# Attention and two dense layers on one core: GpSimd is taken out of layer 1's second product, tiles are lent to whoever comes first

## The chip, the cores and the metric

The kernel runs on one core of a Trainium2 chip. The metric is the device time of one execution in microseconds (us), as the median of a few runs. TensorE (PE, with its weight loads as PEld), VectorE (DVE), ScalarE (ACT), GpSimd (POOL) and the DMA queue that SyncE (SP) feeds work side by side, each through its own list of instructions in a fixed order, with semaphores between them.

## The reference

```
scores = q @ k.T / 8, plus a decay from the running sum of log f, causal mask
x  = softmax(scores) @ v            # 4 batches, 8 heads, 576 rows, 64 columns -> x is 2304 x 512
h  = x @ w_in;   g  = max(0.01 h, h)       # layer 1: w_in 512 x 2048
x1 = g @ w_out                             # layer 1's second product: w_out 2048 x 512
h2 = x1 @ wi2;   g2 = h2 * sigmoid(h2)     # layer 2, same shapes
out = g2 @ wo2
```

The four weights come as 64-bit floats and are turned into 32-bit ones on the chip.

## The kernel before, in words

Each product is made in a split form: an fp32 operand becomes a rounded high part (a copy on ACT) and a low part, operand minus high part (a subtraction), and three matmuls sum high*high, high*low and low*high. The three products behind layer 1's first one also use Strassen's scheme with seven products, numbered q = 1 to 7, so that sums and differences of quarters ("mixes") are made ahead of the split.

No order is written out by hand. A planner (class Plan) runs the kernel's generators in an estimated time: each step asks for an engine with an estimated cost and a rank, each engine takes the waiting step of the lowest rank, and each issue adds one instruction to that engine's list. What two engines can do goes to the one that the planner expects to be done first (either, L137); engines "pd" means POOL or DVE, "d" DVE alone. A subtraction of over 256 columns on POOL is issued as two pieces (less, L337). The chip then works through the lists; only the data decide the waits.

The stretch that the change touches, layer 1's second product, is made of these parts:

- quarters (L1048) loads quarters of g from DRAM (`gq<-g_d`). made (L1088) forms the sums for q 5 and 6 on them (`gq<-gq`, L1328 or, on POOL, L1327), with X_ON the engines of the first. prep (L1099) copies the high part on ACT (L1126) into a tile `gs` and subtracts the low part on DVE (L348), through four `gs` tiles in turn; PE's product reads them (`acc<-gs,w`, L1193, 12 matmuls for each of the 84 `gs`). The three groups of 768 rows are n = 0, 1, 2.
- fills (L1865) loads mixed weights from DRAM (`w<-w_d`, L1882), copies the high part (L1883) and subtracts the low part, `w<-w`, L348 on DVE or L344 on POOL. fills(0) is layer 1's w_out, fills(1) layer 2's wi2, fills(2) its wo2.
- fetch2 (L1841), second_weights (L1896) and combos (L1854) load the raw layer-2 weights (`wst`), turn them into fp32 on ACT and DVE (L1679 to L1683), mix them on DVE (`f<-f`, L1328) in one of two tiles `f`, and store them (`w_d<-f`, L1907). The raw tiles are three `stg` tiles.
- second_input (L1331) loads x1 for layer 2's first product (`x1s`, in an `f` tile, and `x1t`, in two `stg` tiles), mixes it and splits it into `xc`, which `m<-xc,w` (L1491) reads. second_values (L1547) does the same for the last product (`m<-w,gc`, L1634).

An `f` or `stg` tile is taken by a running number (take, L208): number i waits until number i - 2, or i - 3, has been given back, so tiles go round in turn.

Of the kernel before, what the change touches and what calls it, by code (L numbers as in the profile page):

```python
# [19 lines left out]
STG_BUFS = 3  # L20
# [7 lines left out]
U_BUFS = 2  # L28
F_BUFS = 2
MM = 0.119  # L30
# [29 lines left out]
SPLITS = 4  # L60
X_ON = "pd"
SET_B = ("h", "h", ("acc", 0), ("acc", 1))
# [25 lines left out]
class Plan:  # L88
# [8 lines left out]
    def __init__(self):  # L97
        self.now, self.count = 0.0, 0
        self.events, self.ready, self.free = [], {}, {}
        self.seen, self.waiting = {}, {}  # L100
        self.taken, self.given, self.queue = {}, {}, {}
        self.dma_free = 0.0
        self.rate = 360e3
        self.filler = {}

    def at(self, t, fn):
# [113 lines left out]
    def give(self, pool, i):  # L220
        self.given[pool, i] = True
        fn = self.queue.pop((pool, i), None)
        if fn:
            fn()

    def par(self, *gens):
        def step(resume):
            left = [len(gens)]

            def one():  # L230
                left[0] -= 1
                if not left[0]:
                    resume()

            for g in gens:
                self.start(g, one)

        return step
# [28 lines left out]
def fused_kernel(ctx, tc, qt, kt, va, vb, ft, w1, wi2, wo2, out):  # L267
# [49 lines left out]

    def stg(shape, dtype, name):
        return main.tile(shape, dtype, tag="stg", name=name, bufs=STG_BUFS)

# [278 lines left out]
    def load_head(n):  # L599
# [32 lines left out]
        i_st = yield take("stg", STG_BUFS)  # L632
        st = stg([128, S + HALF[1][1]], F32, "qk")
        q2, k2 = st[:, S:S + tn], st[:, 0:ke]
# [573 lines left out]

    last = {}
    split_last = NG * 7 * SF - SPLITS  # L1210

    def sums(n, j, held):
# [35 lines left out]
        if n < NG - 1:  # L1248
            i_u = yield take("u", U_BUFS)
            u = w2t["a"].tile([128, TB], F32, tag="u", name="u", bufs=U_BUFS)  # L1250
        else:
            if j == 0:
                i_u = yield take("f", F_BUFS)
                last["u"] = w2t["b"].tile([128, 2, TB], F32, tag="f", name="us", bufs=F_BUFS)
                signal("last_u")
            yield wait("last_u")
            u = last["u"][:, j]
# [26 lines left out]
        if n < NG - 1:  # L1284
            give("u", i_u)
        elif j == 0:
            yield wait(("x1", n, 0, 3))
            give("f", i_u)

# [41 lines left out]
    def second_input():  # L1331
        yield wait("decoded")
        for g in range(NG):
            yield wait("decoded", *[("x1", g, i, c) for i in range(2) for c in range(KC)])
            if g:
                yield wait(("m", NP * g - STAGE_LEAD[g - 1], 7))
            i_f = yield take("f", F_BUFS)
            signal(("col", g))
            col = w2t["b"].tile([128, 2, 2, TB], F32, tag="f", name="x1s", bufs=F_BUFS)
            a11, a21 = col[:, 0], col[:, 1]  # L1340
            st, st_i = {}, {}

            def load(dst, c, k):
# [4 lines left out]
            def right(k):  # L1348
                st_i[k] = yield take("stg", STG_BUFS)
                st[k] = stg([128, 2, TB], F32, "x1t")  # L1350
                yield from load(st[k], 1, k)

            def split(q, src, done=None):
                t, back = yield from x_room(q)
                xc[g, q] = t, back
                rank = 0 if g or q != 7 else -2
                yield act(2 * TB, lambda: nc.scalar.copy(t[:, 0], src), rank, 0.09)
                yield less(2 * TB, t[:, 1], src, f32(t[:, 0]), "d", rank, PE_LAT)
                if done is not None:
                    give("stg", done)  # L1360
                signal(("xc", g, q))
# [24 lines left out]
            yield wait(*[("xc", g, q) for q in QO])  # L1386
            give("f", i_f)

# [158 lines left out]
    def second_values():  # L1547
        order = [(*tiles2[n], jp) for jp in range(NP // 2) for n in range(2)]
        order += [(*tiles2[n], jp) for n in range(2, len(tiles2)) for jp in range(NP // 2)]
        loaded = {}  # L1550

        def loads2():
            for k in order:
                g, th, jp = k
                yield wait(("g2", g, 2 * jp), ("g2", g, 2 * jp + 1), "wo2_made", ("col", NG - 1))
                i = yield take("f", F_BUFS)
                f = w2t["b"].tile([128, 7, HW], F32, tag="f", name="g2", bufs=F_BUFS)
                yield dma(524e3, lambda: nc.sync.dma_start(
                    out=f[:, 0:4].rearrange("p s (a t) -> p s a t", a=2),
                    in_=g2_d[g, jp, :, :, :, th * 128:(th + 1) * 128]))  # L1560
                loaded[k] = f, i
                signal(("f2", *k))

        p.start(loads2())
        yield wait(("xc", NG - 1, QO[-1]))
        for k in order:
            yield wait(("f2", *k))
            yield from value_combos(*k, *loaded.pop(k))
# [3 lines left out]
    def value_combos(g, th, jp, f, i):  # L1572
# [29 lines left out]
        def back():  # L1602
            yield wait(*[("gc_split", g, th, jp, m) for m in (0, 2, 4, 6)])
            give("f", i)

# [86 lines left out]
    def room(f):  # L1692
# [7 lines left out]
        if where in ("ring0", "ring1"):  # L1700
            t = main.tile(shape, I32, tag=where, name="wsr", bufs=RING_BUFS)
        elif where == "g":
            t = main.tile(shape, I32, tag="g", name="wsg", bufs=G_BUFS)
        elif where == "stg":
            t = stg(shape, I32, "wst")
        else:
            t = slot(where, shape, I32, "wss")
# [133 lines left out]
    def fetch2():  # L1841
        for which in range(2):
            if which:
                yield wait(("m1", NG - 1, 1, 2))
            for j in range(NP):
                for e in range(2):
                    i_st = yield take("stg", STG_BUFS)
                    st = stg([128, DM, 2], I32, "wst")
                    yield dma(524e3, lambda: nc.sync.dma_start(
# [4 lines left out]
    def combos(which, j, f):  # L1854

        y = f[:, 4:6].rearrange("p s n -> p (s n)")
        for e in range(2):
# [3 lines left out]
            yield from to_f32(t, st, y, t, 2, True)  # L1861
            give("stg", i_st)
        yield from mix(f, 2 - which, 2)

    def fills(which):  # L1865
        for u in range(NU):
# [12 lines left out]
            def fill(u, at_, t):  # L1879
# [3 lines left out]
                yield act(2 * HW, lambda: nc.scalar.copy(t[:, :, 0], src), rank)  # L1883
                yield less(2 * HW, t[:, :, 1], src, f32(t[:, :, 0]), "pd", rank, PE_LAT)
                if which == 0:
# [10 lines left out]
    def second_weights():  # L1896
# [3 lines left out]
        def line(which, todo):  # L1900
            while todo:
                j = todo.pop(0)
                yield wait(("words2", which, j, 0))
                i = yield take("f", F_BUFS)
                f = w2t["b"].tile([128, 7, HW], F32, tag="f", name="f", bufs=F_BUFS)
                yield from combos(which, j, f)
# [3 lines left out]
                signal(("spilt", which + 1, j))  # L1910
                give("f", i)

        for which in range(2):
            todo = list(range(NP))
            yield par(*[line(which, todo) for _ in range(F_BUFS)])
        signal("wo2_made")
# [10 lines left out]
    def opening():  # L1927
        first_row["i"] = yield take("stg", STG_BUFS)
        first_row["tile"] = stg([H, 2, HALF[0][1]], F32, "cfr")
        for i in range(5):  # L1930
# [67 lines left out]
```

## Time and profile before

| | before |
|---|---|
| median of three runs | 974.35 us (973.66 to 976.08) |
| profiled execution, its own time | 974.26 us |
| its span, first to last instruction | 972.6 us |
| granted TensorE clock, mean of the span | 0.995 |

In the profile an engine's idle time before an instruction is put down to what released it. Stretches of the span: attention and layer 1's first product to about 392 us (its last matmuls run on to 423 between the others), layer 1's second product from 392 to 619, layer 2's first product from 582 to 794, its second from 794 to 965.

### The profile page before, as it was taken

How to read it: one execution, taken by the hardware profiler on the slowest of the kernel's cores; microseconds unless marked ns; L12 is line 12 of the kernel's file. 1: busy time of each engine (PE TensorE's matmuls, PEld its weight loads, DVE VectorE, ACT ScalarE, POOL GpSimd, SP SyncE). 2: the span in 40 equal slices, each digit the busy share in tenths (PEclk: the TensorE clock that was granted, in tenths of full speed). 3: DMA queues.
4: the chain of work that ended last, by engine and by line, in shares of the span. 5: the costliest groups of instructions: out<-in, count | busy, mean ns of one | idle time of the engine just before them, and what ended most of it. 6: DMA issues, size and time to landing. Idle time of an engine off the chain costs nothing.

```text
span 972.6 us, 18370 instructions
## 1 busy us (share of the span) xinstructions
PE 943.0 (97%) x6483; PEld 891.2 (92%) x6483; DVE 765.3 (79%) x1752; ACT 609.6 (63%) x1382; POOL 127.1 (13%) x126
## 2 busy tenths in 40 slices
PE   9999999999999999899999988999999999999998
PEld 7777998989888989898989978999999999999998
DVE  5998786699689952889899889666656588888885
ACT  6978787788588843665445456456566675444442
POOL 2001220121023100324020157000000020000000
PEclk9999999999999999999999999999999999999999
DMA  7852553466777557894967563695877883544442
GB/s 178 268 174 87 161 172 91 134 229 214 238 235 248 183 184 261 289 375 130 325 216 242 172 219 109 208 335 171 309 273 243 282 266 114 152 131 136 144 122 77
DMA packets 160024, 196.81 MB, mean 202 GB/s; under 512 B 9638, under 2 KB 145982, under 8 KB 159900
## 3 DMA queue, kind: packets, MB, share of 16 engines
q1 hardware_dynamic: 159500, 195.24, 62.8%
q8 instruction: 51, 0.84, 0.4%
q10 hardware_dynamic: 432, 0.39, 0.1%
q14 instruction: 41, 0.34, 0.1%
HBM read 125.94 MB, written 69.65 MB: 201 GB/s over the span
## 4 chain that ended last, share of the span: by engine, by line
PE 71%; DVE 13%; DMA 7%; ACT 4%; issue 3%; SPq 1%; POOL 0%; DVEq 0%; ACTq 0%; POOLq 0%
PE m L1491 18%; PE m L1634 18%; PE hpw L935 12%; PE acc L1193 11%; PE sps L718 4%; PE av L867 4%; PE tps L799 3%; DVE gs L348 2%; DMA gq<-g_d 2%; DVE gq L1328 2%; DVE sc L698 1%; ACT sc L741 1%; PE hps L935 1%; DMA wsr<-in_w_dram 1%; ACT sc L751 1%
## 5 line engine op out<-in xcount | busy, mean ns | idle before, releaser
L935 PE MATMUL hpw<-ring,w 128*128 128x320 f32 (+1 forms) x1344 | 217.4, 303 | 0.1
L1193 PE MATMUL acc<-gs,w 128*128 128x384 f32 x1008 | 187.0, 344 | 13.2 <-DVE gs L348 6.4
L1193 PEld LDWEIGHTS acc<-gs,w 128*128 128x128 f32 x1008 | 180.7, 191 | 16.9 <-DVE gs L348 8.1
L935 PEld LDWEIGHTS hpw<-ring,w 128*128 128x128 f32 x1344 | 190.4, 190 | 2.4 <-issue 1.4
L1491 PE MATMUL m<-xc,w 128*128 128x384 f32 x1008 | 181.4, 340 | 3.8 <-ACT ev L1234 2.0
L1491 PEld LDWEIGHTS m<-xc,w 128*128 128x128 f32 x1008 | 178.1, 188 | 5.4 <-ACT ev L1234 2.3
L1634 PE MATMUL m<-w,gc 128*128 128x256 f32 x1512 | 178.6, 280 | 0.0
L1634 PEld LDWEIGHTS m<-w,gc 128*128 128x128 f32 x1512 | 178.4, 188 | 0.0
L333 ACT CAST gc<-g 128x512 fp32r<-128x512 f32 (+1 forms) x180 | 80.6, 490 | 86.1 <-DVE g L1328 54.9
L1126 ACT CAST gs<-gq 128x768 fp32r<-128x768 f32 x84 | 69.4, 836 | 72.1 <-DVE gq L1328 35.8
L741 ACT ACTIVATE sc<-sc,st 128x576 f32<-128x576 f32 (+4 forms) x160 | 92.9, 581 | 24.8 <-DVE st L698 23.9
L348 DVE TENSOR_TENSOR gs<-gq,gs 128x768 fp32r<-128x768 f32 x84 | 89.8, 1079 | 21.2 <-ACT gs L1126 20.6
L344 POOL TENSOR_TENSOR w<-w 128x256 fp32r<-128x256 f32 x50 | 60.0, 1227 | 296.1 <-ACT w L1883 296.1
L348 DVE TENSOR_TENSOR gc<-g,gc 128x512 fp32r<-128x512 f32 (+1 forms) x180 | 91.3, 532 | 3.2 <-ACT gc L333 2.1
L698 DVE CUSTOM_DVE_ANT_0 sc<-sps,zmask 128x288 f32<-128x288 f32 (+4 forms) x160 | 71.0, 448 | 28.5 <-PE sps L718 21.2
L344 POOL TENSOR_TENSOR m<-qk,m 64x288 fp32r<-64x288 f32 (+1 forms) x56 | 50.3, 909 | 276.1 <-ACT m L333 129.1
L1328 DVE TENSOR_TENSOR g<-g 128x256 f32<-128x256 f32 x144 | 59.3, 421 | 17.9 <-DMA g<-g_d 17.3
L799 PE MATMUL tps<-ident,sc 66*107 66x66 f32 (+3 forms) x480 | 68.5, 269 | 3.5 <-ACT sc L751 1.9
L718 PE MATMUL sps<-m,s 66*128 66x288 f32 (+9 forms) x288 | 66.8, 313 | 2.1 <-DVE st L698 1.4
L799 PEld LDWEIGHTS tps<-ident,sc 66*107 66x107 f32 (+3 forms) x480 | 55.0, 151 | 11.3 <-ACT sc L751 3.9
L1028 ACT ACTIVATE gw<-hpw 128x320 f32<-128x320 f32 (+1 forms) x112 | 44.6, 408 | 27.9 <-PE hpw L935 24.0
L1883 ACT CAST w<-w 128x512 fp32r<-128x512 f32 x84 | 50.6, 618 | 10.2 <-DMA w<-w_d 9.7
(126 smaller groups left out, 1179.8 us busy)
## 6 DMA issues: line engine op xcount, KB each, us to landing
w<-w_d SPq DMA_DIRECT2D x84, 256.0 KB
gq<-g_d SPq DMA_DIRECT2D x48, 384.0 KB
g_d<-z SPq DMA_DIRECT2D x24, 768.0 KB
g<-g_d SPq DMA_DIRECT2D x36, 512.0 KB
w_d<-f SPq DMA_DIRECT2D x16, 896.0 KB
g_d<-gw SPq DMA_DIRECT2D x32, 320.0 KB
wst<-in_w_dram SPq DMA_DIRECT2D x17, 512.0 KB
g_d<-gw SPq DMA_DIRECT2D x32, 256.0 KB
```

What stands on the lines that cost most here:

```text
L333: ("act", act_cost(n, base), lambda: nc.scalar.copy(dst, src), 0.0),
L344: nc.gpsimd.tensor_tensor(dst[:, s_], a[:, s_], b[:, s_], op=ALU.subtract)
L348: ("dve", dve_cost(n), lambda: nc.vector.tensor_tensor(dst, a, b, op=ALU.subtract), 0.0),
L698: yield dve(w, lambda: nc.vector.tensor_tensor_reduce(out=sc[0:qn, k0:k0 + w], in0=ps[0:qn], in1=zmask[0:qn, z0:z0 + w], scale=-0.125, sca ...
L718: nc.tensor.matmul(ps[0:qn], ht[x][:, qs], ht[y][:, k0:k0 + w], start=r == 0, stop=r == len(ops) - 1)
L741: yield act(kn, lambda: nc.scalar.activation(sc[0:qn, 0:kn], sc[0:qn, 0:kn], ACTF.Exp, scale=-1.0, bias=st[0:qn, 2 * i + a:2 * i + a + 1], ...
L799: nc.tensor.transpose(ps[0:k1 - k0, o:o + qn], ht["p"][i][0:qn, k0:k1], ident[0:qn, 0:qn])
L935: nc.tensor.matmul(dst, w[:, wi, c * 128:(c + 1) * 128], x(xi, c), start=(first_ and c == 0 and r == 0), stop=(c == KC - 1 and r == 2), sk ...
L1193: nc.tensor.matmul(dst, w[:, e, wi, j * 128:(j + 1) * 128], x[:, xi, e], start=start and s == 0 and e == 0 and r == 0, stop=stop and s == ...
L1328: ("dve", dve_cost(n), lambda: nc.vector.tensor_tensor(dst, a, b, op=op_), 0.0),
L1491: nc.tensor.matmul(dst, w[:, wi, c * 128:(c + 1) * 128], x[:, xi, c], start=start and c == 0 and r == 0, stop=stop and c == 1 and r == 2, ...
L1634: nc.tensor.matmul(banks[b][:, e], t[:, gi, a * 128:(a + 1) * 128], w[:, wi], start=begin and a == 0 and r == 0, stop=jp == NP // 2 - 1 an ...
```

## The change

- POOL gets no work behind attention: X_ON and the subtraction in fills become "d".
- The two `f` tiles and, behind attention, the three `stg` tiles get a name of their own each, and a new pair lend / back gives any free one to the first who asks.
- Raw wo2 (fetch2, which = 1) is loaded from the point where q 3 of group 0's `xc` is split, instead of from q 2 of group 2's product.
- second_input for group 0 starts only when q 5 of group 2's product is done (INPUT_AT); groups 1 and 2 keep `x1t` in the tile of the fourth `gs` slot.
- second_values waits for all seven `xc` of the last group instead of the last one.

```
-F_BUFS = 2
-X_ON = "pd"
+INPUT_AT = 5
+X_ON = "d"
...
+    def lend(self, pool, keys):
+        def step(resume):
+            free, queue = self.lent.setdefault(pool, (list(keys), []))
+            if free:
+                resume(free.pop(0))
+            else:
+                queue.append(resume)
+        return step
+
+    def back(self, pool, key):
+        free, queue = self.lent[pool]
+        if queue:
+            queue.pop(0)(key)
+        else:
+            free.append(key)
...
-    def stg(shape, dtype, name):
-        return main.tile(shape, dtype, tag="stg", name=name, bufs=STG_BUFS)
+    def stg(i, shape, dtype, name):
+        return main.tile(shape, dtype, tag=f"stg{i % STG_BUFS}", name=name)
+
+    def own(shape, dtype, name):
+        k = yield p.lend("stg2", range(STG_BUFS))
+        return stg(k, shape, dtype, name), lambda: p.back("stg2", k)
...
+    def mixed(shape, name):
+        k = yield p.lend("f", range(2))
+        return w2t["b"].tile(shape, F32, tag=f"f{k}", name=name), lambda: p.back("f", k)
...
     def second_input():
         yield wait("decoded")
         for g in range(NG):
+            if g == 0:
+                yield wait(("m1", NG - 1, 0, INPUT_AT))
...
-            i_f = yield take("f", F_BUFS)
+            col, i_f = yield from mixed([128, 2, 2, TB], "x1s")
...
+            if g:
+                st["x1t"] = tagged(9, [128, 2, 2, TB], F32, "x1t")
...
-                st_i[k] = yield take("stg", STG_BUFS)
-                st[k] = stg([128, 2, TB], F32, "x1t")
+                if g:
+                    st[k], st_i[k] = st["x1t"][:, k], None
+                else:
+                    st[k], st_i[k] = yield from own([128, 2, TB], F32, "x1t")
...
-        yield wait(("xc", NG - 1, QO[-1]))
+        yield wait(*[("xc", NG - 1, q) for q in QO])
...
     def fetch2():
         for which in range(2):
             if which:
-                yield wait(("m1", NG - 1, 1, 2))
+                yield wait(("xc", 0, 3))
             for j in range(NP):
                 for e in range(2):
-                    i_st = yield take("stg", STG_BUFS)
-                    st = stg([128, DM, 2], I32, "wst")
+                    st, i_st = yield from own([128, DM, 2], I32, "wst")
...
-                yield less(2 * HW, t[:, :, 1], src, f32(t[:, :, 0]), "pd", rank, PE_LAT)
+                yield less(2 * HW, t[:, :, 1], src, f32(t[:, :, 0]), "d", rank, PE_LAT)
```

The other places where an `f` tile is taken (us, g2, f) go through mixed in the same way.

The order of PE stays as it was but for one group of six L1193 matmuls that moves ahead of the first L1491 group. What moves is shown at three places. The changed kernel is some 30 lines longer: its L373 is L348 of before, L1357 is L1328, L1713, L1714 and L1716 are L1680, L1681 and L1683, L1091, L1376, L1914 and L1255 are L1066, L1344, L1882 and L1225, L1567 is L1533.

DVE at the beginning of layer 1's second product (`gq<-gq` are the sums of quarters, `w_5656` is the first filled weight, which PE's first product needs), before and then now:

```order
L348 TENSOR_TENSOR gs<-gq,gs 128x768 x4
L1328 TENSOR_TENSOR gq<-gq 128x768 x6
L1680 TENSOR_SCALAR f<-f 128x512
L1681 SCALAR_TENSOR_TENSOR f<-f 128x512
L348 TENSOR_TENSOR w_5656<-w_5656 128x2x256
L1683 SCALAR_TENSOR_TENSOR f<-wst,f 128x512
```

```order
L373 TENSOR_TENSOR gs<-gq,gs 128x768 x4
L1357 TENSOR_TENSOR gq<-gq 128x768 x8
L373 TENSOR_TENSOR w_5656<-w_5656 128x2x256
L1713 TENSOR_SCALAR f<-f 128x512
L1714 SCALAR_TENSOR_TENSOR f<-f 128x512
L373 TENSOR_TENSOR w_5663<-w_5663 128x2x256
```

DVE has eight sums here instead of six and two on POOL, and the first weight's subtraction stands right behind them.

SP around the loads of x1 for group 0 (`x1s`, `x1t`; `x_d<-u` is group 1's last store of x1, `w_d<-f` a store of mixed wi2), before and then now:

```order
L1849 DMA wst<-in_wi_dram 128x1024
L1344 DMA x1s<-x_d 128x2x384 x2
L1907 DMA w_d<-f 128x1792
L1066 DMA gq<-g_d 128x2x384 x2
L1225 DMA x_d<-ev 128x384
```

```order
L1255 DMA x_d<-u 128x384 x2
L1091 DMA gq<-g_d 128x2x384 x3
L1914 DMA w_7237<-w_d 128x2x256
L1091 DMA gq<-g_d 128x2x384
L1914 DMA w_7255<-w_d 128x2x256
L1914 DMA w_7273<-w_d 128x2x256
L1376 DMA x1s<-x_d 128x2x384 x2
L1376 DMA x1t<-x_d 128x2x384 x2
L1914 DMA w_7291<-w_d 128x2x256
```

The four loads now stand behind the last `gq` load and behind the first wi2 weights, some twenty rows later, in one piece.

DVE around the last `gs` subtractions (`w_7341` and so on are wi2 weights, `z<-m,z` is layer 2's first product), before and then now:

```order
L1328 TENSOR_TENSOR x1t<-x1t,x1s 128x768
L348 TENSOR_TENSOR gs<-gq,gs 128x768
L348 TENSOR_TENSOR xc<-x1s,xc 128x768
L348 TENSOR_TENSOR w_7543<-w_7543 128x2x256
L348 TENSOR_TENSOR gs<-gq,gs 128x768
L348 TENSOR_TENSOR xc<-x1t,xc 128x768 x2
L348 TENSOR_TENSOR w_7582<-w_7582 128x2x256
```

```order
L1357 TENSOR_TENSOR x1t<-x1t,x1s 128x768
L373 TENSOR_TENSOR gs<-gq,gs 128x768
L373 TENSOR_TENSOR xc<-x1s,xc 128x768
L373 TENSOR_TENSOR gs<-gq,gs 128x768
L373 TENSOR_TENSOR w_7320<-w_7320 128x2x256
L373 TENSOR_TENSOR w_7341<-w_7341 128x2x256
L373 TENSOR_TENSOR w_7360<-w_7360 128x2x256
L373 TENSOR_TENSOR xc<-x1t,xc 128x768 x2
L373 TENSOR_TENSOR w_7377<-w_7377 128x2x256
```

Half of the subtractions that POOL did before now stand on DVE ahead of its last `gs`, and half behind it.

## Rows read from the trace of the kernel before

**Rows 1.** The page: busy time by engine, and the chain that ended last.
```profile
PE 943.0 (97%) x6483; PEld 891.2 (92%) x6483; DVE 765.3 (79%) x1752; ACT 609.6 (63%) x1382; POOL 127.1 (13%) x126
...
PE 71%; DVE 13%; DMA 7%; ACT 4%; issue 3%; SPq 1%; POOL 0%; DVEq 0%; ACTq 0%; POOLq 0%
```

**Rows 2.** Windows: stretch and length, engines' busy us (x instructions), clock, DMA share, GB/s.
```profile
392.00:423.00 31.00, 27.11 (x164) 26.77 (x164) 26.21 (x40) 18.50 (x35) 4.63 (x5) 0.94 0.93 306
423.00:451.00 28.00, 26.15 (x146) 25.25 (x144) 25.29 (x25) 18.98 (x31) 15.69 (x12) 1.00 0.66 239
451.00:495.00 44.00, 40.70 (x216) 39.55 (x216) 39.61 (x58) 21.14 (x33) 5.19 (x2) 0.96 0.74 245
495.00:575.00 80.00, 79.94 (x452) 79.84 (x453) 70.90 (x90) 42.06 (x63) 10.51 (x9) 1.00 0.72 232
575.00:619.00 44.00, 36.07 (x190) 34.17 (x189) 39.47 (x40) 26.80 (x44) 26.07 (x21) 0.96 0.36 111
619.00:794.00 175.00, 174.99 (x1000) 174.35 (x999) 111.79 (x201) 108.87 (x208) 3.24 (x4) 1.00 0.81 272
794.00:972.60 178.60, 174.60 (x1485) 174.40 (x1484) 148.26 (x346) 80.00 (x182) 2.08 (x2) 1.00 0.44 131
...
567.00:608.40 41.40, 33.47 (x176) 31.85 (x175) 41.29 (x36) 26.24 (x44) 32.38 (x26) 0.96 0.46 140
```

**Rows 3.** Timeline of PE, 370 to 630: start, length, instructions [idle before <-releaser].
```profile
396.52 1.65 PE L1193 MATMUL acc<-gs,w 128*128 128x384 f32 x4 [3.49 <-DVE w L348]
...
451.33 33.97 PE L1193 MATMUL acc<-gs,w 128*128 128x384 f32 x191 [1.77 <-DVE gs L348]
486.57 0.44 PE L1193 MATMUL acc<-gs,w 128*128 128x384 f32 x1 [1.26 <-ACT gs L1126]
...
577.00 2.38 PE L1193 MATMUL acc<-gs,w 128*128 128x384 f32 x12 [1.11 <-DVE gs L348]
580.95 1.14 PE L1193 MATMUL acc<-gs,w 128*128 128x384 f32 x5 [1.57 <-DVE gs L348]
...
584.10 1.97 PE L1491 MATMUL m<-xc,w 128*128 128x384 f32 x5 [1.83 <-DVE xc L348]
...
594.68 8.74 PE L1193 MATMUL acc<-gs,w 128*128 128x384 f32 x48 [1.44 <-ACT ev L1264]
605.40 1.33 PE L1491 MATMUL m<-xc,w 128*128 128x384 f32 x6 [1.97 <-ACT ev L1234]
```

**Rows 4.** Groups: busy us, mean ns of one; 374.8 to 608.4, then three of 495:535.
```profile
L348 DVE TENSOR_TENSOR gs<-gq,gs 128x768 fp32r<-128x768 f32 x84 | 89.8, 1079 | 21.2 <-ACT gs L1126 20.6
L1328 DVE TENSOR_TENSOR gq<-gq 128x768 f32<-128x768 f32 x43 | 49.4, 1173 | 4.9 <-DMA gq<-g_d 4.6
L348 DVE TENSOR_TENSOR w<-w 128x512 fp32r<-128x512 f32 x29 | 22.8, 804 | 4.4 <-ACT w L1883 4.1
...
L344 POOL TENSOR_TENSOR w<-w 128x256 fp32r<-128x256 f32 x44 | 54.7, 1271 | 110.6 <-ACT w L1883 110.6
...
L348 DVE TENSOR_TENSOR gs<-gq,gs 128x768 fp32r<-128x768 f32 x22 | 20.7, 954 | 2.2 <-ACT gs L1126 1.9
L1328 DVE TENSOR_TENSOR gq<-gq 128x768 f32<-128x768 f32 x8 | 7.4, 951 | 0.0
...
L348 DVE TENSOR_TENSOR w<-w 128x512 fp32r<-128x512 f32 x2 | 1.4, 685 | 0.0
```

**Rows 5.** Timeline 436 to 457, DVE and then POOL.
```profile
445.23 1.49 DVE L348 TENSOR_TENSOR gs<-gq,gs 128x768 fp32r<-128x768 f32 x1
...
450.33 0.95 DVE L348 TENSOR_TENSOR gs<-gq,gs 128x768 fp32r<-128x768 f32 x1
...
438.37 10.35 POOL L344 TENSOR_TENSOR w<-w 128x256 fp32r<-128x256 f32 x8 [4.09 <-ACT w L1883]
```

**Rows 6.** DVE's timeline from 384, and a piece of the chain from 450.
```profile
386.06 8.74 DVE L1328 TENSOR_TENSOR gq<-gq 128x768 f32<-128x768 f32 x6 [4.64 <-DMA gq<-g_d]
...
454.78 4.94 DMA gq<-g_d
```

More of the change, by code (lines that the diff above doesn't have):

```diff
@@ L104, in __init__ @@
         self.filler = {}
+        self.lent = {}
     def at(self, t, fn):
@@ L632, in load_head @@
         i_st = yield take("stg", STG_BUFS)
-        st = stg([128, S + HALF[1][1]], F32, "qk")
+        st = stg(i_st, [128, S + HALF[1][1]], F32, "qk")
         q2, k2 = st[:, S:S + tn], st[:, 0:ke]
@@ L1252, in sums @@
             if j == 0:
-                i_u = yield take("f", F_BUFS)
-                last["u"] = w2t["b"].tile([128, 2, TB], F32, tag="f", name="us", bufs=F_BUFS)
+                last["u"], i_u = yield from mixed([128, 2, TB], "us")
                 signal("last_u")
@@ L1287, in sums @@
             yield wait(("x1", n, 0, 3))
-            give("f", i_u)
+            i_u()
     tiles2 = [(g, th) for g in range(NG) for th in range(TB // 128)]
@@ L1336, in second_input @@
                 yield wait(("m", NP * g - STAGE_LEAD[g - 1], 7))
-            i_f = yield take("f", F_BUFS)
+            col, i_f = yield from mixed([128, 2, 2, TB], "x1s")
             signal(("col", g))
-            col = w2t["b"].tile([128, 2, 2, TB], F32, tag="f", name="x1s", bufs=F_BUFS)
             a11, a21 = col[:, 0], col[:, 1]
             st, st_i = {}, {}
+            if g:
+                st["x1t"] = tagged(9, [128, 2, 2, TB], F32, "x1t")
             def load(dst, c, k):
@@ L1359, in split @@
                 if done is not None:
-                    give("stg", done)
+                    done()
                 signal(("xc", g, q))
@@ L1386, in second_input @@
             yield wait(*[("xc", g, q) for q in QO])
-            give("f", i_f)
+            i_f()
     sets_n = [0]
@@ L1555, in loads2 @@
                 yield wait(("g2", g, 2 * jp), ("g2", g, 2 * jp + 1), "wo2_made", ("col", NG - 1))
-                i = yield take("f", F_BUFS)
-                f = w2t["b"].tile([128, 7, HW], F32, tag="f", name="g2", bufs=F_BUFS)
+                f, i = yield from mixed([128, 7, HW], "g2")
                 yield dma(524e3, lambda: nc.sync.dma_start(
@@ L1603, in back @@
             yield wait(*[("gc_split", g, th, jp, m) for m in (0, 2, 4, 6)])
-            give("f", i)
+            i()
         p.start(back())
@@ L1704, in room @@
         elif where == "stg":
-            t = stg(shape, I32, "wst")
+            t = stg(i, shape, I32, "wst")
         else:
@@ L1861, in combos @@
             yield from to_f32(t, st, y, t, 2, True)
-            give("stg", i_st)
+            i_st()
         yield from mix(f, 2 - which, 2)
@@ L1903, in line @@
                 yield wait(("words2", which, j, 0))
-                i = yield take("f", F_BUFS)
-                f = w2t["b"].tile([128, 7, HW], F32, tag="f", name="f", bufs=F_BUFS)
+                f, i = yield from mixed([128, 7, HW], "f")
                 yield from combos(which, j, f)
@@ L1910, in line @@
                 signal(("spilt", which + 1, j))
-                give("f", i)
+                i()
         for which in range(2):
             todo = list(range(NP))
-            yield par(*[line(which, todo) for _ in range(F_BUFS)])
+            yield par(*[line(which, todo) for _ in range(2)])
         signal("wo2_made")
@@ L1928, in opening @@
         first_row["i"] = yield take("stg", STG_BUFS)
-        first_row["tile"] = stg([H, 2, HALF[0][1]], F32, "cfr")
+        first_row["tile"] = stg(first_row["i"], [H, 2, HALF[0][1]], F32, "cfr")
         for i in range(5):
```

## The prediction

> **What bounds the kernel now.** I read the page first: PE is busy for 97% of the span, and the chain that ended last is 71% PE and 13% DVE [rows 1]. So time can only be won where PE stops, or runs slowly. The windows by stage say where [rows 2]; the reader should compare PE's busy time with the length. From 619 to 794 PE is busy for 174.99 of 175 us, and from 794 on only the end of the kernel is open. From 392 to 619, layer 1's second product, it lacks 3.89, 1.85, 3.30, 0.06 and 7.93 us in the five windows, 17.0 in all. Three of these windows also have a granted clock of 0.94 to 0.96, which is a piece at 1.2 instead of 2.4 GHz: 0.06 of 31, 0.04 of 44 and 0.04 of 44 us, some 5.4 us of lost clock, each time in a window in which PE had stopped. 17.0 + 5.4 = 22.4 us is all that can be won there; an order of PE that hardly changes cannot win elsewhere.
>
> Next PE's timeline, for who ends the stops [rows 3]: nearly all are ended by DVE (first `w`, then `gs`, `xc`), a few by ACT. Behind 567 the reason is plain: DVE is busy for 41.29 of 41.40 us, while PE lacks 7.93 in the window of 44 [rows 2]. DVE is the bound there.
>
> Last, why DVE is so full. In the groups a `gs` subtraction takes 1079 ns on the mean of the stretch and 954 between 495 and 535, where POOL does nothing; a `gq` sum 1173 against 951, a `w` subtraction 804 against 685 [rows 4]. The timeline shows the switch: POOL runs eight pieces back to back from 438.37 to 448.72; a `gs` of DVE takes 1.49 us inside that and 0.95 right behind it [rows 5]. POOL's reads slow DVE. The excess is 84 x 0.125 = 10.5, 43 x 0.222 = 9.5 and 29 x 0.119 = 3.5 us, 23.5 us of DVE's time in the stretch.
>
> **The rule weighed against it.** The rows give a price for a collision: about half a microsecond for one DVE instruction (1.49 - 0.95), and 23.5 us in all [rows 4, 5]. The Trainium skill, "SBUF — State Buffer", section "Who interferes with whom", says that a DVE instruction with two SBUF inputs contends with a GpSimd instruction that reads SBUF, and that the shared port pair is an exclusive lock: the loser fully blocks until the other's instruction ends. That there is contention, the rows confirm; blocked for POOL's mean piece of 1.271 us, 44 times, DVE would lose 56 us, and the relief would be more than PE's stops can return. The rows show less than half of it, and the sum goes by them.
>
> **The change part by part**, against the profiled execution's own 974.26 us (median 974.35, so the two stand for each other).
>
> *Off POOL.* In the stretch POOL does 44 pieces, that is 22 `w` subtractions [rows 4], and 5 `gq` sums (its other 5 instructions of 49). All go to DVE, at 0.685 and 0.951 us [rows 4]: 15.1 + 4.8 = 19.9 us, against 23.5 us of excess that goes. But the order puts only 11 of the 22 ahead of the last `gs`: 7.5 + 4.8 = 12.3 us. It also draws some ten short `f` instructions of wi2 ahead of it, at most 0.685 each, 6.9. So DVE's work ahead of the last `gs` falls by 4 us at least; I take 6 to 8, since `x1s`, `x1t` and `xc` instructions had an excess too. Three more `w` subtractions between 785 and 800 go to DVE: 2.1 us, hidden behind PE's own 174.6 us, DVE being busy for 148.26 of 178.60 [rows 2]; without that cover 2.1 us.
>
> *First stop* (3.49 before 396.52, ended by `w` [rows 3]). DVE makes six `gq` in 8.74 us from 386.06 [rows 6], two of them beside POOL's, then two `f` instructions, then `w`. Now it is eight sums and `w`: 386.06 + 8 x 0.951 + 0.685 = 394.4, so PE goes on 2.1 us earlier. Of the clock loss, 1.9, I take half: 0.9.
>
> *Second and third* (1.85 in 423 to 451, 3.30 and 1.8 of clock in 451 to 495 [rows 2]). Around 445 DVE gets rid of eight POOL pieces and takes up `w` subtractions of its own that other work hid. I take 1.4 of 1.85. At 486 two POOL sums ran beside DVE, but `gq` loads (4.94 us for one in the chain [rows 6]) and an ACT copy have a part too, and these stay: 1.5 of 3.30, and 0.9 of the clock.
>
> *The end, 567 to 619.* Ahead of the last `gs` the order leaves 13 `gs`, 6 `gq`, 9 sums and splits of x1 of the same size, 7 `w` and two short ones: 28 x 0.954 + 7 x 0.685 + 2 x 0.55 = 32.6 us for DVE, where it needed 41.3. PE's own work there is 33.5 [rows 2], so DVE is just no longer the bound. The stops before 577.00, 580.95 and 584.10 (4.5 us) should go, and those by ACT's copies (1.44 and 1.97 [rows 3]) shrink, since ACT stands behind a cast that waits for slow `gs`. I take 6.0 of 7.93 and 1.3 of 1.8 of clock.
>
> *x1 loaded later.* The four loads of `x1s` and `x1t` now stand behind the last `gq` loads, and DVE's first sum of x1 stands ahead of the last eleven `gs`. If they land late, DVE waits with those `gs` behind it, and PE for DVE. Nothing at the least; at most about the 4.94 us of a load of the same size [rows 6] and as much again behind the others, 10. I take 2, nearer the lower end, since all of x1 that they read but group 1's last store is long in place, and DVE gets there with time that it has won.
>
> *Lent tiles, wo2 later, the wait for all seven `xc`.* No instruction is added. Their cover is PE's unbroken run from 619 on, and DVE's 63 idle us of 175 there [rows 2]; wo2 is needed from 794. Nothing, unless wo2 comes late, which its 175 us exclude for all but a gross error.
>
> Sum: 2.1 + 0.9 + 1.4 + 1.5 + 0.9 + 6.0 + 1.3 - 2.0 = 12.1 us; 974.3 - 12.1 = **962 us**. From 619 on PE has no stop that could give the gain back. What is late next are `gq` loads and ACT's copies.
>
> **The rivals.**
> - *x1 late.* As forecast, but the late loads cost 8 us instead of 2: 968 us. For it: the stops at 577 to 584 are just where they land. Against it: from 575 to 619 the DMA engines are busy for 0.36 of the time, the least of the stretch [rows 2], so a load meets a free queue.
> - *Everything goes.* With DVE no longer slowed, all stops and the clock return: 974.3 - 22.4 = 952 us. Against it: the third stop has other causes, and a stop removed early lets PE ask earlier for what comes later.
> - *PE's stops are held by something else* (loads, the fixed order of ACT): DVE gets shorter and idles instead, 972 us, no difference. For it: three of the eight stops are put down to ACT [rows 3].
> - *DVE becomes the bound: slower.* If the long DVE times were not POOL's doing, nothing is relieved, and DVE carries 12.3 + 6.9 = 19.2 us more. It idles for some 21 us between 392 and 575, and not at all behind 567 [rows 2]; with half of it paid, 984 us. It decides if `gs` keeps a mean above 1.08 us with POOL idle. Against it: the 0.95 right behind POOL's end [rows 5]. The Trainium skill, "Perfetto Trace Analysis", section "Optimizing Scalar/DVE Operations", speaks for this side: where DVE is saturated, it says, work may be moved off it, to GpSimd even, and this change does the reverse; it adds itself that the shared port may void this, and the rows say so.
>
> **How the numbers follow.** Forecast 0.55, x1 late 0.21, everything goes 0.10, held by something else 0.08, slower 0.06. A measurement of this kernel tells 0.3%, 2.9 us, from no change. The first three are faster: 0.86; the fourth is the same: 0.08; the last slower: 0.06. The forecast's terms, each between nothing and all of its stop, reach from about 955 to 968. The range of 954 to 970 takes in x1 late and leaves out the two cases at the upper end (0.14) and a part of the one at 952.
>
> **What would show it.** POOL's busy time ends with attention. In the stretch `gs`, `gq` and `w` have means near 0.954, 0.951 and 0.685 us. PE goes on before 395 instead of at 396.5; its stops from 575 to 619 add up to under 2 us instead of 7.93; the clock shows fewer pieces at 0.5; PE is unbroken behind. It is wrong if `gs` stays above 1.08, if PE waits for `xc` or `gs` while DVE waits for `x1s`, or if PE stops anywhere behind 619.

## The result, and the profile after

| | before | after |
|---|---|---|
| median | 974.00 us (973.32 to 976.08, 4 runs) | 960.21 us (958.04 to 963.02, 4 runs) |
| profiled execution, its own time | 974.26 us | 963.02 us |
| its span | 972.6 us | 961.3 us |

The ratio is 0.985 (95% interval 0.9823 to 0.9877): faster by 13.8 us, where 12.1 had been forecast, and inside the range.

Busy time and the chain on the page of the changed kernel, to be held against [rows 1]:

```profile
PE 940.9 (98%) x6483; PEld 891.6 (93%) x6483; DVE 753.1 (78%) x1782; ACT 610.8 (64%) x1382; POOL 56.5 (6%) x71
...
PE 68%; DVE 13%; DMA 9%; ACT 5%; issue 3%; SPq 2%; POOL 0%; DVEq 0%; ACTq 0%; POOLq 0%
```

POOL has lost 70.6 us of work, and DVE, which took all of it over, is busy for 12.2 us *less* than before. That one comparison already says that DVE's time before was not all work.

The groups of DVE from 374.8 to 600, for [rows 4]:

```profile
L373 DVE TENSOR_TENSOR gs<-gq,gs 128x768 fp32r<-128x768 f32 x84 | 79.4, 952 | 17.5 <-ACT gs L1151 16.9
L1357 DVE TENSOR_TENSOR gq<-gq 128x768 f32<-128x768 f32 x48 | 44.1, 950 | 5.7 <-DMA gq<-g_d 5.6
L373 DVE TENSOR_TENSOR w<-w 128x512 fp32r<-128x512 f32 x45 | 29.7, 684 | 4.9 <-ACT w L1915 4.9
```

`gs` fell from 1079 to 952 ns, `gq` from 1173 to 950, `w` from 804 to 684.

Windows by stage, for [rows 2] (length, busy us of PE, PEld, DVE, ACT, POOL, then clock, DMA share, GB/s):

```profile
392.00:423.00 31.00, 30.13 (x190) 29.55 (x189) 24.85 (x43) 20.51 (x39) 0.00 (x0) 1.00 1.02 354
423.00:451.00 28.00, 27.03 (x154) 26.70 (x153) 27.37 (x38) 20.50 (x33) 0.00 (x0) 1.00 0.66 236
451.00:495.00 44.00, 40.88 (x218) 39.66 (x217) 39.69 (x62) 21.46 (x32) 0.00 (x0) 0.96 0.75 247
495.00:575.00 80.00, 77.86 (x431) 77.40 (x431) 69.85 (x96) 40.61 (x60) 0.00 (x0) 0.98 0.69 231
575.00:607.00 32.00, 31.97 (x180) 31.32 (x180) 31.99 (x46) 26.05 (x45) 0.00 (x0) 1.00 0.59 186
```

Layer 1's second product now ends near 607 instead of 619. What PE lacks there is 0.87 + 0.97 + 3.12 + 2.14 + 0.03 = 7.1 us, where it lacked 17.0. The last row is the one to stop at: DVE is busy for 31.99 of 32 us, as full as ever, and PE lacks 0.03 us. A full engine is not a bound as long as what it makes comes in time.

PE's timeline, the stops over 0.5 us between 386 and 620, all of them, for [rows 3]:

```profile
394.10 0.97 PE L1218 MATMUL acc<-gs,w 128*128 128x384 f32 x4 [0.86 <-DVE w L373]
...
445.76 34.33 PE L1218 MATMUL acc<-gs,w 128*128 128x384 f32 x192 [0.97 <-DVE gs L373]
481.06 4.41 PE L1218 MATMUL acc<-gs,w 128*128 128x384 f32 x23 [0.97 <-DVE gs L373]
486.33 0.44 PE L1218 MATMUL acc<-gs,w 128*128 128x384 f32 x1 [0.85 <-ACT gs L1151]
...
488.07 59.15 PE L1218 MATMUL acc<-gs,w 128*128 128x384 f32 x324 [1.30 <-DVE gs L373]
549.36 29.16 PE L1218 MATMUL acc<-gs,w 128*128 128x384 f32 x155 [2.14 <-DVE gs L373]
```

Two readings. All stops of [rows 3] behind 495 are gone. And there is one that before did not have, 2.14 us ahead of 549.36, with a lower clock behind it. DVE's timeline shows what stands ahead of the late `gs`:

```profile
540.14 2.82 DVE L1357 TENSOR_TENSOR gq<-gq 128x768 f32<-128x768 f32 x3 [0.94 <-DMA gq<-g_d]
543.07 0.96 DVE L373 TENSOR_TENSOR gs<-gq,gs 128x768 fp32r<-128x768 f32 x1
543.95 3.56 DVE L1357 TENSOR_TENSOR gq<-gq 128x768 f32<-128x768 f32 x4
547.43 1.01 DVE L1309 TENSOR_TENSOR u<-acc,u 128x384 f32<-128x384 f32 x2
548.36 0.94 DVE L373 TENSOR_TENSOR gs<-gq,gs 128x768 fp32r<-128x768 f32 x1
```

The sums of group 2 begin late, at 540.14, and waited for a load; then four sums and two `u` sums stand ahead of the `gs` that PE wants. Windows of PE's row alone (length, busy, clock, DMA share, GB/s) price the clock:

```profile
300.00:310.00 10.00, 10.00 (x63) 0.83 0.71 223
544.00:555.00 11.00, 8.86 (x41) 0.84 0.23 71
```

The second costs 0.16 x 11 = 1.8 us, so the new stop is worth 3.9. The first lies in attention, ahead of everything that the change moves, and the second profile of this kernel (below) has 1.00 there; it costs this execution about 1.7 us (0.17 x 10), and is part of why it is the longest of the four.

### The profile page after: what moved, and what is told of

Same layout as the page of the kernel before. It is cut to its first block, busy times and chain, and to the rows that moved or that the text cites. A ratio compares the mean times of both kernels' runs of the same rounds, so it can differ in the third digit from the quotient of the medians.

```text
span 961.3 us, 18261 instructions
## 1 busy us (share of the span) xinstructions
PE 940.9 (98%) x6483; PEld 891.6 (93%) x6483; DVE 753.1 (78%) x1782; ACT 610.8 (64%) x1382; POOL 56.5 (6%) x71
## 4 chain that ended last, share of the span: by engine, by line
PE 68%; DVE 13%; DMA 9%; ACT 5%; issue 3%; SPq 2%; POOL 0%; DVEq 0%; ACTq 0%; POOLq 0%
PE m L1667 18%; PE m L1525 18%; PE acc L1218 10%; PE hpw L960 10%; PE sps L743 4%; PE av L892 4%; PE tps L824 3%; DMA gq<-g_d 3%; DVE gq L1357 2%; DMA wst<-in_wi_dram 2%; ACT sc L766 1%; DVE sc L723 1%; DVE gs L373 1%; ACT sc L776 1%; PE hps L960 1%
## 5 line engine op out<-in xcount | busy, mean ns | idle before, releaser
L373 DVE TENSOR_TENSOR gs<-gq,gs 128x768 fp32r<-128x768 f32 x84 | 79.4, 952 | 17.5 <-ACT gs L1151 16.9
L373 DVE TENSOR_TENSOR gc<-g,gc 128x512 fp32r<-128x512 f32 (+1 forms) x180 | 89.8, 525 | 3.3 <-ACT gc L358 1.9
L1357 DVE TENSOR_TENSOR g<-g 128x256 f32<-128x256 f32 x144 | 58.3, 418 | 16.7 <-DMA g<-g_d 16.2
L373 DVE TENSOR_TENSOR w<-w 128x512 fp32r<-128x512 f32 x84 | 55.6, 686 | 14.6 <-ACT w L1915 14.4
```

The lines of the kernel that those rows point to most:

```text
L373: ("dve", dve_cost(n), lambda: nc.vector.tensor_tensor(dst, a, b, op=ALU.subtract), 0.0),
L1357: ("dve", dve_cost(n), lambda: nc.vector.tensor_tensor(dst, a, b, op=op_), 0.0),
```

## The experiments

Theory A: the gain is that POOL's reads no longer slow DVE. Theory B: it is the rest of the change, that is the order of work with x1 and wo2 loaded later and tiles lent. Rival C: DVE's long times had another cause than POOL. Times are medians; the ratio is against runs of the kernel before on the same chip.

**1. POOL off alone.** The kernel before, with two edits:

```
-X_ON = "pd"
+X_ON = "d"
-                yield less(2 * HW, t[:, :, 1], src, f32(t[:, :, 0]), "pd", rank, PE_LAT)
+                yield less(2 * HW, t[:, :, 1], src, f32(t[:, :, 0]), "d", rank, PE_LAT)
```

> The kernel before with one part of the change: the gq sums and the w subtractions may only go to DVE; the tiles go round in turn as before, x1 and wo2 are loaded as early as before. Theory A (the gain is POOL's reads gone from beside DVE): gs, gq and w at 0.95, 0.95 and 0.69 us, PE goes on at 394 at the first stop, no stop of note from 575 to 607, and the time is that of the changed kernel, 960 us, within 3. Theory B (the gain is the later x1 and wo2 and the tiles lent out): 974, or 971 at best.

Measured: 957.16 us, ratio 0.983 (0.9808 to 0.9852). Theory A, and all of the gain, with 3 us to spare. From 495 to 607 PE has no stop over 0.2 us in it (length, busy of PE, PEld, DVE, ACT, POOL):

```profile
495.00:575.00 80.00, 79.83 (x451) 79.19 (x450) 70.02 (x90) 46.67 (x72) 0.00 (x0) 1.00 0.68 214
575.00:607.00 32.00, 32.00 (x180) 31.37 (x180) 28.63 (x45) 19.22 (x34) 0.00 (x0) 1.00 0.42 127
```

**2. All but POOL off.** The changed kernel, with the same two lines set back to "pd".

> The changed kernel with that one part taken back: gq sums and w subtractions may go to POOL again; tiles lent, x1 and wo2 later. Theory A: gs, gq and w slow again (means over 1.05, 1.1 and 0.75 us), some 8 us of stops at the end of layer 1's second product, 974 us, within 3. Theory B: 960 to 963.

Measured: 978.20 us, ratio 1.0039 (1.0021 to 1.0057): not faster, but slower by 3.8 us. DVE's groups from 374.8 to 619:

```profile
L373 DVE TENSOR_TENSOR gs<-gq,gs 128x768 fp32r<-128x768 f32 x82 | 87.3, 1074 | 12.1 <-ACT gs L1151 12.0
L1357 DVE TENSOR_TENSOR gq<-gq 128x768 f32<-128x768 f32 x42 | 48.5, 1178 | 6.4 <-DMA gq<-g_d 6.1
L373 DVE TENSOR_TENSOR w<-w 128x512 fp32r<-128x512 f32 x32 | 27.1, 862 | 4.7 <-ACT w L1915 4.5
```

`gs` and `gq` are back at the means of [rows 4], and `w` is above its own there (862 against 804). With run 1 this divides the change: POOL off is worth about 17 us, the rest costs about 4. Theory B falls, and by more than A asked for: 974 had been expected.

**3. The collision by itself.** Nothing is taken off DVE; POOL reads the same weights beside it, and what it makes goes into a small tile that nobody reads:

```
+                    if which < 2 and u % 2:
+                        for k in range(2):
+                            nc.gpsimd.tensor_tensor(spare, src_hi[:, k], src_hi[:, k], op=ALU.subtract)
```

> The changed kernel, every list of DVE, ACT and PE as it is; beside every second w subtraction of DVE, POOL subtracts the high part of the same w tile from itself, in two pieces of 128x256, into a small tile that nobody reads (some 40 pieces in the stretch, as many as POOL had there before). Nothing is taken off DVE, so this shows the collision alone. Theory A: each piece costs DVE about 0.5 us, some 20 us in the stretch; gs's mean rises above 1.0 us, PE stops again at the end of the stretch, 968 to 976 us. Rival C (DVE's times are long for another reason than POOL, such as what DVE reads at the time): gs stays at 0.95 and the time at 960.

Measured: 978.73 us, ratio 1.005 (1.0031 to 1.0069), some 18 us above the changed kernel, and above the range given. The page's first line, with DVE's 1782 instructions in the order that they have in the changed kernel:

```profile
PE 946.2 (97%) x6483; PEld 894.8 (92%) x6483; DVE 774.9 (79%) x1782; ACT 611.3 (63%) x1382; POOL 113.2 (12%) x127
```

Against 753.1, DVE is busy for 21.8 us more with not one instruction more, by 56 pieces of POOL: 0.39 us for each. DVE's and POOL's timelines from 428, where the collisions are dense:

```profile
431.10 1.10 DVE L1716 SCALAR_TENSOR_TENSOR f<-wst,f 128x512 int32<-128x512 int32 x1
432.12 1.36 DVE L373 TENSOR_TENSOR gs<-gq,gs 128x768 fp32r<-128x768 f32 x1
433.40 3.14 DVE L1920 TENSOR_TENSOR w<-w 128x512 fp32r<-128x512 f32 x3
436.46 1.36 DVE L373 TENSOR_TENSOR gs<-gq,gs 128x768 fp32r<-128x768 f32 x1
...
442.73 0.94 DVE L373 TENSOR_TENSOR gs<-gq,gs 128x768 fp32r<-128x768 f32 x1
...
430.98 6.03 POOL L1923 TENSOR_TENSOR spare<-w 128x256 bf16<-128x256 f32 x6 [0.96 <-ACT w L1916]
```

A `gs` takes 1.36 us while POOL reads and 0.94 behind it. PE stops four times between 432 and 451 (1.55, 1.96, 1.40 and 2.13 us) and again for 2.30 at 593.82. Rival C falls.

**4. POOL only writes.** The same number of pieces of the same size, as zeros that are overwritten before use:

```
+                if which < 2 and u % 2:
+                    for k in range(2):
+                        nc.gpsimd.memset(f32(t[:, k, 0]), 0.0)
```

> The same number of POOL pieces of the same size, but they only write: POOL fills the high half of the same w tiles with zeros ahead of the copy that overwrites it. Theory A in the narrow form (two engines' reads collide): gs at 0.95 us, 960 us, within 3. In the broad form (any work of POOL slows DVE): gs above 1.0 and 966 to 976.

Measured: 961.31 us, ratio 0.9879 (0.9857 to 0.9902). The groups of DVE and of POOL from 374.8 to 619:

```profile
L373 DVE TENSOR_TENSOR gs<-gq,gs 128x768 fp32r<-128x768 f32 x82 | 77.5, 952 | 12.3 <-ACT gs L1151 12.0
L373 DVE TENSOR_TENSOR w<-w 128x512 fp32r<-128x512 f32 x56 | 36.5, 684 | 4.9 <-ACT w L1918 4.8
```
```profile
L1916 POOL MEMSET w<- 128x256 f32 x54 | 14.9, 309 | 255.4 <-PE acc L1218 171.7 <-PE hpw L960 75.5 <-DMA w<-w_d 8.2
```

`gs` and `w` are where they are with POOL idle, to the nanosecond. The zeros take less time than the subtractions (0.309 us), so this is a smaller dose; but eleven of the `gs` run beside one, and none of these takes more than 0.96 us. One DVE instruction did pay for a write: a TENSOR_SCALAR of 128x512 with one input took 0.62 us beside two of these pieces, at 405.36, where all others take 0.41 to 0.43. For `gs` and `w` it is POOL's reads, not POOL at work. The Trainium skill, "SBUF — State Buffer", section "Who interferes with whom", states just this, that a DVE instruction with two SBUF inputs contends with a GpSimd instruction that reads SBUF and not with one that only writes it; runs 3 and 4 agree, 1.36 and 0.952 us for a `gs`.

**5. and 6. The change and POOL off alone, side by side on one chip.**

> The changed kernel itself once more, beside the next three on one chip, since taking POOL off alone gave 957.2 us and the whole change 960.2 on another chip. If the rest of the change (tiles lent, x1 and wo2 later) costs something, this stays 2 to 4 us above the next run; if the difference was the chip's, both agree within 1.5 us.

> The kernel before with only POOL's work behind attention given to DVE, once more. 957 us if the rest of the change costs about 3 us by the new stop of 2.1 us at 549 and the clock behind it, which this kernel's trace does not have; 959 to 960 if the difference was the chip's.

Measured: 959.96 us (ratio 0.9861, 0.9842 to 0.9879) and 956.34 us (0.9826, 0.9807 to 0.9845). Of the 3.6 us between them 3.0 were there in the first pair as well, so the chip did not make them. In the second profile of the change the new stop is there again, and in POOL off alone PE runs on for 85 us:

```profile
545.18 29.18 PE L1218 MATMUL acc<-gs,w 128*128 128x384 f32 x155 [2.15 <-DVE gs L373]
```
```profile
486.31 85.33 PE L1193 MATMUL acc<-gs,w 128*128 128x384 f32 x473 [1.30 <-DVE gs L348]
```

**7. x1 early.** The changed kernel, less

```
-            if g == 0:
-                yield wait(("m1", NG - 1, 0, INPUT_AT))
```

> The changed kernel without the wait for q 5 of group 2 ahead of x1's loads for group 0, so that x1 is loaded about as early as before; tiles still lent, wo2 still later. If the late x1 is what brings the new stop at 549 (work of wi2 drawn ahead in its place), the stop goes and the time is 957; if the lent tiles are (two 896 KB stores of mixed wi2 weights stand in the queue among the gq loads), the stop stays and the time is that of the change.

Measured: 959.89 us, ratio 0.9846 (0.9823 to 0.9869). The stop stays, in two parts of 1.05 and 1.56 us at 543.33 and 547.27. So loading x1 later neither costs nor brings anything that this run can tell. What is left is wi2. Ahead of the sums of group 2 DVE does 80 `f` instructions in the trace of the change and 70 in that of POOL off alone (run 1). The ten are the last of the eight pieces in which wi2 is mixed, 5.2 us at the 0.42 and 0.68 us that they take, and the piece's 896 KB store follows them. (The next two expectations call the last piece a quarter; it is an eighth.)

The time of the ten on DVE does not by itself explain the stop. Behind the last of them, which ends at 529.04, DVE idles for 4.9 us until the sums begin; its timeline has most of it:

```profile
530.84 0.96 DVE L373 TENSOR_TENSOR gs<-gq,gs 128x768 fp32r<-128x768 f32 x1 [0.75 <-ACT gs L1151]
532.59 0.69 DVE L373 TENSOR_TENSOR w<-w 128x512 fp32r<-128x512 f32 x1 [0.79 <-ACT w L1915]
...
536.01 0.69 DVE L373 TENSOR_TENSOR w<-w 128x512 fp32r<-128x512 f32 x1 [1.74 <-ACT w L1915]
```

What the sums wait for at 540.14 is a load of `gq`. It was issued at 531.82, while the piece's store was on its way (529.38 to 538.08), and landed 8.3 us later; in run 1 the store before it had landed, and the load took 5.3 us. DVE's list is another one, too: 39 sums stand ahead of the `gs` that PE wants, and 37 in run 1. That the store and the order of the list, rather than the ten instructions, made the stop is a reading of the trace; the next two runs move all three together.

**8. The last piece of wi2 mixed later.** The changed kernel, with

```
+                if which == 0 and j == NP - 1:
+                    yield wait(("m1", NG - 1, 0, 7))
```

ahead of the `f` tile in second_weights.

> The changed kernel with one wait more: the mixing of the last quarter of wi2 (ten f instructions of DVE and one 896 KB store) starts only when q 7 of group 2's product is done, so that it stands behind the sums of group 2, as it does in the kernel with POOL off alone. If these instructions and that store, drawn ahead by the tiles lent and the later x1, make the new stop of 2.1 us at 545 to 549, the stop goes, with the clock behind it, and the time is 956 to 957. If the stop has another cause, 960.

Measured: 969.30 us, ratio 0.9939 (0.9916 to 0.9963). A miss in the time, but not in the stop: from 495 to 575 PE is busy for 80.00 of 80 us. A much larger one took its place:

```profile
605.57 0.69 PE L1525 MATMUL m<-xc,w 128*128 128x384 f32 x1 [10.06 <-ACT xc L1391]
```

The DMA queue's timeline has the reason:

```profile
556.82 0.97 SPq L1376 DMA_DIRECT2D x1s<-x_d  x2
557.84 0.47 SPq L1376 DMA_DIRECT2D x1t<-x_d  x1
...
600.73 0.37 SPq L1376 DMA_DIRECT2D x1t<-x_d  x1
```

The raw words of that piece lay in two of the three `stg` tiles until they were mixed, so one `x1t` got its tile 43 us later. A tile lent to whoever comes first goes to whoever holds it longest, too.

**9. The last piece of wi2 loaded later.** The same wait, put ahead of the load in fetch2 instead:

> The changed kernel with the last quarter of raw wi2 loaded only when q 7 of group 2's product is done. In the run that held back the mixing alone, the stop at 545 went as expected, but a new one of 10.06 us at 605 came: the raw words lay in two of the three stg tiles until they were mixed, so one x1t load was issued at 600.73 instead of 558, and the xc that PE wanted came late. Here the stg tiles stay free for x1t. If that reading is right, both stops are gone, both x1t loads are issued by 566, and the time is 956 to 957, that of POOL off alone. If the stop at 605 came from the late mixing itself, it stays and the time is near 969.

Measured: 957.38 us, ratio 0.9818 (0.9788 to 0.9848). The stop at 545 and run 8's at 605 are gone (one of 0.61 us, put down to ACT, is new), and both `x1t` loads leave together:

```profile
485.02 86.25 PE L1218 MATMUL acc<-gs,w 128*128 128x384 f32 x479 [1.30 <-DVE gs L373]
577.36 9.86 PE L1218 MATMUL acc<-gs,w 128*128 128x384 f32 x54 [0.61 <-ACT ev L1293]
```
```profile
556.88 0.97 SPq L1376 DMA_DIRECT2D x1s<-x_d  x2
557.89 0.98 SPq L1376 DMA_DIRECT2D x1t<-x_d  x2
```

From the first `acc<-gs,w` matmul to the end of the last the profiles have 210.1 us here, 210.2 and 210.0 in POOL off alone, and 214.2 and 211.9 in the change. So what the rest of the change cost hung on this one piece. The three that follow go for the stops that are left, on top of POOL off alone.

**10. Sums and subtractions first.** Rank -1 instead of 0 for the sum for q 6 and for the subtraction of `gs`.

> POOL off alone, and in addition the rank of the sums for q 6 and of the low-part subtractions of gs set ahead of everything else of DVE. It aims at the stops that are left: 0.97, 0.87 and 1.30 us at 477 to 484 and the clock behind them (about 1.7 us), where DVE makes sums for later slices and the u sums ahead of a gs that PE waits for. If DVE's order makes them, up to 4.8 us go: 953 to 955. If they come from DVE's rate there (two sums and a subtraction for each gs, 2.85 us, against 2.1 us of PE), they only move: 957.

Measured: 960.69 us, ratio 0.9869 (0.9851 to 0.9888), 4.4 us worse than run 6 and above both times expected. The stops moved, and grew: 0.83, 0.79, 0.84, 1.66 and 1.59 us between 477 and 491. An order by rank does not help where DVE has too much to do in that place.

**11. Group 1 in the order 1, 5, 6.** POOL off alone, with

```
-    ((1, -2), (6, 1), (5, 2), (2, 3), (7, 4), (4, 6), (3, 7)),
+    ((1, -2), (5, 1), (6, 2), (2, 3), (7, 4), (4, 6), (3, 7)),
```

> POOL off alone, and group 1 takes its products in the order 1, 5, 6 instead of 1, 6, 5. In order 6, 5 each of the first gs behind q 1 needs two sums and a subtraction of DVE, 2.85 us against PE's 2.1; in order 5, 6 each needs one sum and one subtraction, 1.9 us. If the stops at 477 to 486 are DVE's rate there (which is what the run with the ranks changed points to, where they only moved), 3.1 us and the clock behind them (about 1.7) go: 952 to 954. If they come from the loads of gq or from ACT's order, 956.

Measured: **953.92 us, ratio 0.9774 (0.9752 to 0.9797)**, the lowest median of this study. In place of the three stops, 3.1 us in all, there is one of 1.64, so half of what was expected came. The granted clock of the window is 1.00 where run 1 has 0.96 (the row of each, 451 to 495: run 1, then this one, PE's alone):

```profile
451.00:495.00 44.00, 40.82 (x218) 39.54 (x217) 39.96 (x63) 20.66 (x30) 0.00 (x0) 0.96 0.80 267
```
```profile
451.00:495.00 44.00, 42.13 (x237) 1.00 0.81 271
```

The clock is not shown to come from the order: the second profile of the change (run 5) has 1.00 in this window with the three stops in place (0.90, 0.86 and 1.30 us).

**12. Group 2 in that order as well.**

> As the run before, with group 2 in the order 1, 5, 6 as well. Group 2 has no stop there with POOL off alone, so nothing more is to be had from it: the same time as the run before, within 1.5 us; above it if the changed order brings work of x1 into a worse place.

Measured: 954.30 us, ratio 0.9786 (0.9764 to 0.9809): no different from run 11, as expected.

## Why the prediction was right, point by point

- **What bounds, and the cause.** Right, and shown: POOL's reads slowed DVE (runs 1 to 4). `gs`, `gq` and `w` came to 0.952, 0.950 and 0.684 us against 0.954, 0.951 and 0.685 forecast.
- **First stop.** 2.1 us and 0.9 of clock were taken; the stop shrank from 3.49 to 0.86 us, 2.6, and the window's clock from 0.94 to 1.00, 1.9. PE went on at 394.10, where 394.4 was forecast: the sums began 0.2 us later than before, at 386.27, and the eight took 7.17 us where 7.6 had been counted. That both executions came to the stretch at the same time is luck; in the second profile of the change PE goes on at 392.12.
- **Second.** 1.4 taken. The window lacks 0.97 instead of 1.85: 0.9.
- **Third.** 1.5 and 0.9 of clock taken; it lacks 3.12 instead of 3.30, and the clock is 0.96 still. Almost nothing came, and the step was mistaken in its reason: the loads and ACT's copies do not hold these stops, DVE's own work does. In order 6, 5 each `gs` needs two sums and a subtraction there, and run 11 takes the stops from 3.1 to 1.64 us by the order alone. Its median is 2.4 us below run 6's, on another chip. The lower clock behind these stops comes in some executions and not in others (0.96 in the first profile of the change, 1.00 in the second).
- **The end.** 6.0 and 1.3 taken. All of the 7.93 went, and the clock is 1.00. The caution, that ACT's copies would keep a part, was not needed: the stops put down to ACT were DVE's too, one step back, since one of 2.30 us is there again in run 3, where POOL reads beside DVE.
- **x1 loaded later.** 2.0 taken as a cost; run 7 shows none. A late `x1t` can stop PE, though: in run 8 one cost 10.06 us. That this is the prediction's upper bound is chance, since there a tile was held, and the load did not stand behind other loads.
- **Lent tiles and wi2.** This step failed. "No instruction is added", cost nothing. But the ten `f` instructions that the prediction itself had counted as drawn ahead (6.9 us at most; 5.2 in the trace) were set against the sum of DVE's work up to the last `gs`, and neither their place, just ahead of group 2's sums, nor the store that comes with them was weighed. Drawn ahead, this piece made the new stop, 2.14 us and 1.8 of clock, and run 9 gives it back. Which part of it did, the instructions, the store ahead of the `gq` load or the order that DVE's list took, stays open; the trace speaks for the last two (run 7).

The sum of what was measured in the first profile: 2.6 + 1.9 + 0.9 + 0.2 + 7.9 + 1.8 - 3.9 = 11.4 us, beside 11.2 between the two profiled executions (974.26 - 963.02). Attention's piece of clock is not in this sum, since the two executions stand nearly level as the stretch begins (the first `acc<-gs,w` at 392.43 and 392.62). Medians differ by 13.8, since the profiled execution of the change is its longest. The forecast's 12.1 was close because errors of opposite sign nearly met: 1.5 us more came at the first stop, 2.4 at the end and 2.0 by x1, 5.9 in all; 0.5 less at the second stop, 2.2 at the third and 3.9 by wi2, 6.6 in all.

The rivals: that everything goes (952) was nearer than it looked, since run 11 stands at 953.9, by leaving the rest of the change out and turning one order; "held by something else" and "slower" are excluded by runs 1 and 3, and "x1 late" by run 7. Raw wo2 loaded later was never run by itself; run 9 keeps it and is level with POOL off alone.

## What to carry to other kernels

Before work is shared out to a second engine, compare the mean of the first engine's instructions inside and outside the second's busy stretches: here 70.6 us of POOL's work were worth less than nothing, and taking them back made DVE's total shorter. When tiles are lent to the first who asks, ask what will come earlier by it, at which place in each engine's and the DMA queue's list, and what will hold a tile while it waits: work that is free on the sum can still stop the critical engine. And where an engine is the bound for a few microseconds only, count its work for each item that the critical engine takes (2.85 us against 2.1), and change the order so that the ratio fits, rather than ranks.

## What the runs showed of the hardware

**Both engines lose in a collision, and the price goes by POOL's instruction.** In run 3 a `gs` beside POOL takes 1.36 instead of 0.95 us, a `w` 1.10 instead of 0.68, a `f` of L1716 1.10 instead of 0.68: the same 0.41 to 0.42, whatever DVE's instruction is. In the kernel before a `gs` pays 0.54 beside POOL's `w` pieces (1.49 [rows 5]) and 1.17 beside POOL's sums of 128x768 (2.12 below). POOL's piece takes 0.614 us in the one case that it ran alone, and 1.03 on the mean. In run 3 a DVE instruction thus waits for some two thirds of a piece of POOL, not for all of POOL's time in the profile. The Trainium skill ("SBUF — State Buffer", "Who interferes with whom") calls the shared port pair an exclusive lock and has the other engine fully block; it writes the second of DVE's two-port modes. Taking POOL's busy time in the profile for the block, as the prediction's 56 us did, counts POOL's own waiting with it.

**The input matters.** The `u` sums of DVE have one input in PSUM. In the kernel before, two of them ran inside a POOL stretch, among instructions with both inputs in SBUF (DVE's timeline, then POOL's):

```profile
487.59 0.55 DVE L1280 TENSOR_TENSOR u<-acc,u 128x384 f32<-128x384 f32 x1
488.05 2.12 DVE L348 TENSOR_TENSOR gs<-gq,gs 128x768 fp32r<-128x768 f32 x1
490.09 0.54 DVE L1280 TENSOR_TENSOR u<-acc,u 128x384 f32<-128x384 f32 x1
490.56 2.11 DVE L1328 TENSOR_TENSOR gq<-gq 128x768 f32<-128x768 f32 x1
...
486.66 5.19 POOL L1327 TENSOR_TENSOR gq<-gq 128x768 f32<-128x768 f32 x2 [37.94 <-DMA gq<-g_d]
```

They take 0.55 and 0.54 us, as one does in run 1 with POOL idle (0.55), while the `gs` between them and the `gq` behind them take over twice their 0.95. The same section of the Trainium skill says so of a DVE instruction with at most one SBUF input outside the two-port modes, and the rows agree.
